# Attention and expert layer on one core: the attention part written out as a fixed order across two batches

## The chip, the core and the metric

The kernel runs on 1 core of one Trainium2 chip. The metric is the device time of one execution in microseconds (us). Four engines matter here: TensorE (PE) multiplies matrices into PSUM, VectorE (DVE) and ScalarE (ACT) work elementwise, and two queues issue transfers (DMA): SyncE's (SP) and GpSimd's (POOL). Each engine runs its own instructions strictly in the order in which they stand, and waits at each one until what it needs is there.

## What is computed

```python
# attention, for each batch b of 8 and head h of 8; 576 positions, 64 values a head
q_p, k_p = phi(q), phi(k)                 # phi(x) = max(x, 0) + exp(min(x, 0))
kv  = einsum('bhsd,bhse->bhde', k_p, v)
z   = sum(k_p, axis=2)
num = einsum('bhsd,bhde->bhse', q_p, kv)
den = einsum('bhsd,bhd->bhs', q_p, z)
x   = (num / den) as a matrix of 4608 x 512
# expert layer: 8 experts, 512 -> 1024 -> 512
P = exp(x @ w_gate)
for _ in range(8):                        # rows and columns made equal in turn
    P /= P.sum(1);  P /= P.sum(0);  P *= N / E
out = sum over e of P[:, e] * (relu(x @ w1[e]) @ w2[e])
```

## The kernel before

The work has three stages. The attention runs batch by batch (the loop at L103). The sinkhorn stage (L231 to L265) computes the 36 x 128 x 8 table of weights. The expert stage (L272 to L313) runs over four pairs of experts and nine blocks of 512 columns, with 16 tiles of `hps` (4 matmuls each) and 8 tiles of `yps` (8 matmuls each) for a block and a pair. The PE order begins the expert stage's `hps` right after the gate's matmuls (`lgps`, L234), between the matmuls of the sinkhorn stage.

Inside a batch the 576 positions stand in five chunks `c`, four of 128 rows and one of 64. This is what happens to a batch:

- SP loads k and q of each chunk (`kn`, `qn`, L134 and L138) in pieces of 256 bytes, POOL loads v (`vn`, L142) and casts it to 16 bits. `kn` and `qn` have 2 buffers, so the load of a chunk waits until DVE has used the chunk two before it. `vn` has 6.
- ACT computes exp(min(x, 0)) in two instructions each for k and q (`tk`, `tq`, L149, L150, L154, L155). DVE adds max(x, 0) (`kp`, `qp`, L151, L156). ACT casts `kp` to 16 bits (`kp16`, L153). PE sums it over the positions (`zps`, L158).
- After the fifth chunk DVE copies `zps` (`z_sb`, L160), PE spreads it over 128 rows (`zbc`, L161, in 32-bit numbers), and DVE normalises q chunk by chunk in four steps: product `jk` (L167), sum `den` (L169), reciprocal `rden` (L170), `qps` (L171).
- For each of four head pairs `i`, PE multiplies k and v (10 matmuls into `kvps`, L182), and DVE copies the two 64 x 64 blocks into `kv2` (L188, L190). `kvps` is one PSUM bank, so the matmuls of pair `i + 1` wait until the copies of pair `i` are done.
- PE transposes `qps` (4 matmuls into `qtr`, L196, one into `qtr4`, L200). ACT copies `qtr` to `qpsT` (L205), DVE copies `qtr4` (L207).
- PE multiplies `kv2` and `qpsT` (8 matmuls into `xps`, L217). ACT copies the tiles of even `i` (L220), DVE those of odd `i` (L223) into `xT`, which the expert stage reads.

The order on each engine is not the order of the code: a scheduler places every instruction by its own estimate of when it can run. It has put only a little of the next batch's `kp` and `qp` between the products of a batch. The weights of the first pair of experts (four loads, `load_pair_weights(0)`, L87) stand first on the POOL queue, ahead of all `vn`.

Of the kernel before, what the change touches and what calls it, by code (L numbers as in the profile page):

```python
# [8 lines left out]
FP32 = mybir.dt.float32  # L9
FP16 = mybir.dt.float16  # L10
A = mybir.AluOpType
# [10 lines left out]
def kernel(  # L22
# [49 lines left out]
    w2t = [w2p.tile([P, 2, NFT, DM], FP16, name=f"w2t{i}", tag="w2t")  # L72
           for i in range(NPAIR)]

    def load_pair_weights(pr):
        e0 = 2 * pr
        for j in range(2):
            nc.gpsimd.dma_start(  # L78
                out=w1t[pr][:, j],
                in_=moe_w1[e0 + j].rearrange("(dc di) f -> di dc f", di=P),  # L80
            )
            nc.gpsimd.dma_start(
                out=w2t[pr][:, j],
                in_=moe_w2[e0 + j].rearrange("(fc fi) d -> fi fc d", fi=P),
            )

    load_pair_weights(0)  # L87

    h_pair = hpp.tile([P, 2, NFT, NBW], FP16, name="h_pair")

# [9 lines left out]
    att = tc.alloc_tile_pool(name="att", bufs=1, side="right")  # L100
    apsum = tc.alloc_tile_pool(name="apsum", bufs=8, space=bass.MemoryType.PSUM)

    for b in range(B):  # L103
        kv2 = [att.tile([P, P], FP16, name=f"kv2_{b}_{i}", tag="kv2", bufs=8)
               for i in range(NHP)]
        qpsT = [att.tile([P, S], FP16, name=f"qpsT_{b}_{i}", tag="qpsT", bufs=8)
                for i in range(NHP)]
        kvps = apsum.tile([P, H, D], FP32, name=f"kvps_{b}", tag="aps")
        zps = apsum.tile([1, DM], FP32, name=f"zps_{b}", tag="aps")
        z_sb = att.tile([1, DM], FP32, name=f"z_sb_{b}", tag="z_sb", bufs=2)  # L110
        zbc = apsum.tile([P, DM], FP32, name=f"zbc_{b}", tag="aps")
        qtr4 = apsum.tile([P, NHP, SLAST], FP32, name=f"qtr4_{b}", tag="aps")

        kp = []
        kp16 = []
        vn = []
        qp = []
        qps = []
        for c in range(NCH):
            kp.append(att.tile([P, DM], FP32, name=f"kp_{b}_{c}", tag="kp", bufs=2))  # L120
            kp16.append(att.tile([P, DM], FP16, name=f"kp16_{b}_{c}", tag="kp16", bufs=6))
            vn.append(att.tile([P, DM], FP16, name=f"vn_{b}_{c}", tag="vn", bufs=6))
            qp.append(att.tile([P, DM], FP32, name=f"qp_{b}_{c}", tag="qp", bufs=6))
            qps.append(att.tile([P, DM], FP32, name=f"qps_{b}_{c}", tag="qps", bufs=6))

        for c in range(NCH):
            pc = P if c < NCH - 1 else SLAST
            s0 = c * P
            kn = att.tile([P, DM], FP32, name=f"kn_{b}_{c}", tag="kn", bufs=2)
            qn = att.tile([P, DM], FP32, name=f"qn_{b}_{c}", tag="qn", bufs=2)  # L130
            tmpk = att.tile([P, DM], FP32, name=f"tk_{b}_{c}", tag="tmpk", bufs=2)
            tmpq = att.tile([P, DM], FP32, name=f"tq_{b}_{c}", tag="tmpq", bufs=2)

            nc.sync.dma_start(  # L134
                out=kn[:pc].rearrange("p (h d) -> p h d", d=D),
                in_=k[b, :, s0 : s0 + pc, :].rearrange("h s d -> s h d"),
            )
            nc.sync.dma_start(  # L138
                out=qn[:pc].rearrange("p (h d) -> p h d", d=D),
                in_=q[b, :, s0 : s0 + pc, :].rearrange("h s d -> s h d"),  # L140
            )
            nc.gpsimd.dma_start(  # L142
                out=vn[c][:pc].rearrange("p (h d) -> p h d", d=D),
                in_=v[b, :, s0 : s0 + pc, :].rearrange("h s d -> s h d"),
            )
            if pc < P:
                nc.vector.memset(kn[pc:], 0.0)
                nc.vector.memset(qn[pc:], 0.0)
            nc.scalar.activation(tmpk, kn, AF.Relu, scale=-1.0)  # L149
            nc.scalar.activation(tmpk, tmpk, AF.Exp, scale=-1.0)  # L150
            nc.vector.scalar_tensor_tensor(out=kp[c], in0=kn, scalar=0.0,  # L151
                                           in1=tmpk, op0=A.max, op1=A.add)
            nc.scalar.activation(kp16[c], kp[c], AF.Copy)  # L153
            nc.scalar.activation(tmpq, qn, AF.Relu, scale=-1.0)  # L154
            nc.scalar.activation(tmpq, tmpq, AF.Exp, scale=-1.0)  # L155
            nc.vector.scalar_tensor_tensor(out=qp[c], in0=qn, scalar=0.0,  # L156
                                           in1=tmpq, op0=A.max, op1=A.add)
            nc.tensor.matmul(zps, ones16f[:pc], kp16[c][:pc],  # L158
                             start=(c == 0), stop=(c == NCH - 1))
        nc.vector.tensor_copy(out=z_sb, in_=zps)  # L160
        nc.tensor.matmul(zbc, ones32[0:1, :], z_sb[0:1, :], start=True, stop=True)  # L161

        for c in range(NCH):
            junk = att.tile([P, H, D], FP32, name=f"jk_{b}_{c}", tag="junk", bufs=2)
            den = att.tile([P, H], FP32, name=f"den_{b}_{c}", tag="den", bufs=2)
            rden = att.tile([P, H], FP32, name=f"rden_{b}_{c}", tag="rden", bufs=2)
            nc.vector.tensor_tensor(out=junk.rearrange("p h d -> p (h d)"),  # L167
                                    in0=qp[c], in1=zbc, op=A.mult)
            nc.vector.tensor_reduce(out=den, in_=junk, axis=AXX, op=A.add)  # L169
            nc.vector.reciprocal(out=rden, in_=den)  # L170
            nc.vector.scalar_tensor_tensor(  # L171
                out=qps[c].rearrange("p (h d) -> p h d", d=D),
                in0=qp[c].rearrange("p (h d) -> p h d", d=D), scalar=KXS,
                in1=rden.unsqueeze(2).to_broadcast([P, H, D]),
                op0=A.mult, op1=A.mult)

        for i in range(NHP):
            for j in range(2):
                hh = 2 * i + j
                for c in range(NCH):  # L180
                    pc = P if c < NCH - 1 else SLAST
                    nc.tensor.matmul(  # L182
                        kvps[:, hh, :],
                        kp16[c][:pc, i * P : (i + 1) * P],
                        vn[c][:pc, hh * D : (hh + 1) * D],
                        start=(c == 0), stop=(c == NCH - 1))
            nc.vector.memset(kv2[i].bitcast(FP32), 0.0)
            nc.vector.tensor_scalar(out=kv2[i][0:D, 0:D], in0=kvps[0:D, 2 * i, :],  # L188
                                    scalar1=0.0, scalar2=None, op0=A.add)
            nc.vector.tensor_scalar(out=kv2[i][D:P, D:P], in0=kvps[D:P, 2 * i + 1, :],  # L190
                                    scalar1=0.0, scalar2=None, op0=A.add)

        for i in range(NHP):
            qtr = apsum.tile([P, (NCH - 1) * P], FP32, name=f"qtr_{b}_{i}", tag="aps")
            for c in range(NCH - 1):
                nc.tensor.matmul(qtr[:, c * P : (c + 1) * P],  # L196
                                 qps[c][:, i * P : (i + 1) * P], idt,
                                 is_transpose=True,
                                 start=(c == 0), stop=(c == NCH - 2))
            nc.tensor.matmul(qtr4[:, i, :],  # L200
                             qps[NCH - 1][:SLAST, i * P : (i + 1) * P],
                             idt[:SLAST, :SLAST],
                             is_transpose=True,
                             start=(i == 0), stop=(i == NHP - 1))
            nc.scalar.activation(qpsT[i][:, 0 : (NCH - 1) * P], qtr, AF.Copy)  # L205
        for i in range(NHP):
            nc.vector.tensor_scalar(out=qpsT[i][:, (NCH - 1) * P : S],  # L207
                                    in0=qtr4[:, i, :],
                                    scalar1=0.0, scalar2=None, op0=A.add)

        for i in range(NHP):
            for sb in range(2):
                n0 = sb * NBW
                nw = NBW if sb == 0 else S - NBW
                xps = apsum.tile([P, nw], FP32, name=f"xps_{b}_{i}_{sb}",
                                 tag="aps")
                nc.tensor.matmul(xps, kv2[i], qpsT[i][:, n0 : n0 + nw],  # L217
                                 start=True, stop=True)
                if i % 2 == 0:
                    nc.scalar.activation(xT[i][:, b * S + n0 : b * S + n0 + nw],  # L220
                                         xps, AF.Copy)
                else:
                    nc.vector.tensor_scalar(  # L223
                        out=xT[i][:, b * S + n0 : b * S + n0 + nw], in0=xps,
                        scalar1=0.0, scalar2=None, op0=A.add)

    att.release()
    apsum.release()
# [115 lines left out]
```

## Time and profile before

| | |
|---|---|
| time, median of 4 runs | 1295.89 us (1294.96 to 1296.31) |
| the profiled execution: time, and its span | 1296.25 us, 1294.1 us |
| PE busy | 1148.2 us, 89% |
| DVE busy | 555.7 us, 43% |
| ACT busy | 359.8 us, 28% |

The span runs from the first to the last instruction; the execution's time holds 2.15 us besides. Shares over the whole span are a mean over unlike stages, so the rows below are taken stage by stage. A line of the profile that begins with a time gives start and duration in us, the engine, the line of the kernel, what is written and read, and how many instructions were merged into it. In square brackets it gives the idle time of the engine just before it and what ended that.

### The profile page before, as it was taken

The numbers are of one execution on the slowest core, as the hardware profiler recorded it, in microseconds if no ns is written. First come the engines' busy times: TensorE is split into PE (matmuls) and PEld (weight loads), VectorE is DVE, ScalarE is ACT, GpSimd is POOL, SyncE is SP. The second block draws the span as 40 slices with busy tenths as digits, with TensorE's granted clock in tenths as the row PEclk, the third lists the DMA queues.
The fourth block names the chain that finished last, engine by engine and source line by source line (L and its number), as shares of the span: only waits on it lengthen the run. The fifth ranks groups of instructions, "written<-read, shape, count | busy, mean of one in ns | idle before, by whom it ended". The sixth has DMA issues, their size and how long they took to land.

```text
span 1294.1 us, 13893 instructions
## 1 busy us (share of the span) xinstructions
PE 1148.2 (89%) x5658; PEld 529.2 (41%) x5658; DVE 555.7 (43%) x973; ACT 359.8 (28%) x627; POOL 48.2 (4%) x63
## 2 busy tenths in 40 slices
PE   0455555679999999999999999999999999999998
PEld 0222222245444444444444444444444444444443
DVE  1677767745333333333333333333334333333333
ACT  2566566521222111222112222112221112221111
POOL 3021111100000000100000001000000000000000
PEclk9999555569999999999999999999999999999999
DMA  9777766400000000520000007000000161000111
GB/s 185 109 96 99 102 105 103 64 1 2 1 1 1 1 1 1 82 49 1 1 1 1 1 1 131 1 1 1 1 1 1 32 119 45 33 33 33 41 49 41
DMA packets 130832, 50.71 MB, mean 39 GB/s; under 512 B 113872, under 2 KB 122064, under 8 KB 130768
## 3 DMA queue, kind: packets, MB, share of 16 engines
q0 software_dynamic: 50576, 21.51, 13.6%
q1 hardware_dynamic: 80192, 28.32, 9.1%
q8 instruction: 44, 0.72, 0.2%
q14 instruction: 20, 0.16, 0.0%
HBM read 61.88 MB, written 9.44 MB: 55 GB/s over the span
## 4 chain that ended last, share of the span: by engine, by line
PE 84%; DVE 8%; DMA 4%; ACT 3%; issue 1%; SPq 0%
PE hps L282 39%; PE yps L298 38%; DMA qn<-in_q_dram 2%; PE qtr L196 2%; DVE jk L167 2%; DVE den L169 2%; DVE qps L171 2%; DMA kn<-in_k_dram 2%; PE zbc L161 1%; PE kvps L182 1%; ACT kp L153 1%; PE xps L217 1%; PE qtr L200 1%; DVE kp L151 1%; PE vps L254 1%
## 5 line engine op out<-in xcount | busy, mean ns | idle before, releaser
L282 PE MATMUL hps<-xT,w1t 128*128 128x512 f16 x2304 | 507.1, 380 | 0.0
L298 PE MATMUL yps<-w2t,h_pair 128*128 128x512 f16 x2304 | 504.0, 379 | 0.4 <-DVE out_acc L304 0.4
L287 ACT ACTIVATE h_pair<-hps 128x512 f16<-128x512 f32 x360 | 214.7, 597 | 778.6 <-PE hps L282 756.8
L298 PEld LDWEIGHTS <-h_pair 128*128 128x128 f16 x2304 | 225.1, 98 | 271.6 <-issue 0.7
L282 PEld LDWEIGHTS <-w1t 128*128 128x128 f16 x2304 | 224.8, 98 | 270.5 <-issue 2.2
L308 DVE SCALAR_TENSOR_TENSOR out_acc<-yps,pnat,out_acc 128x512 f32<-128x512 f32 x252 | 189.2, 751 | 246.3 <-PE yps L298 246.3
L289 DVE TENSOR_SCALAR h_pair<-hps 128x512 f16<-128x512 f32 x216 | 149.2, 691 | 333.7 <-PE hps L282 333.6
L158 PE MATMUL zps<-kp,ones16f 128*1 128x512 f16 (+1 forms) x40 | 21.0, 581 | 79.0 <-ACT kp L153 79.0
L196 PE MATMUL qtr<-idt,qps 128*128 128x128 f32 x128 | 43.9, 447 | 43.4 <-DVE qps L171 41.5
L196 PEld LDWEIGHTS qtr<-idt,qps 128*128 128x128 f32 x128 | 22.7, 204 | 54.7 <-DVE qps L171 47.9
L205 ACT ACTIVATE qpsT<-qtr 128x512 f16<-128x512 f32 x32 | 19.1, 597 | 84.6 <-PE qtr L196 84.6
L182 PE MATMUL kvps<-vn,kp 128*128 128x64 f16 (+1 forms) x320 | 34.3, 239 | 8.8 <-DVE kv L190 8.8
L304 DVE TENSOR_SCALAR out_acc<-yps,pnat 128x512 f32<-128x512 f32 x36 | 26.9, 750 | 33.7 <-PE yps L298 33.7
L142 POOL DMA_DIRECT2D vn<-in_v_dram x40 | 33.6, 865 | 208.9 <-PE kvps L182 199.1
L182 PEld LDWEIGHTS <-kp 128*128 128x128 f16 (+1 forms) x320 | 26.1, 124 | 31.9 <-issue 23.2
L151 DVE SCALAR_TENSOR_TENSOR kp<-kn,tk 128x512 f32<-128x512 f32 x40 | 27.2, 681 | 23.8 <-ACT tk L150 23.6
L156 DVE SCALAR_TENSOR_TENSOR qp<-qn,tq 128x512 f32<-128x512 f32 x40 | 27.3, 682 | 18.5 <-ACT tq L155 18.2
L78 POOL DMA_DIRECT2D w1t<-in_moe_w_dram x8 | 6.1, 763 | 749.0 <-PE hps L282 749.0
L158 PEld LDWEIGHTS <-ones16f 128*1 128x1 f16 (+1 forms) x40 | 3.1, 91 | 74.6 <-issue 72.3
L167 DVE TENSOR_TENSOR jk<-qp,zbc 128x512 f32<-128x512 f32 x40 | 25.9, 681 | 9.8 <-PE zbc L161 9.8
L149 ACT ACTIVATE tk<-kn 128x512 f32<-128x512 f32 x40 | 24.9, 622 | 17.5 <-DMA kn<-in_k_dram 17.5
L154 ACT ACTIVATE tq<-qn 128x512 f32<-128x512 f32 x40 | 24.9, 624 | 14.6 <-DMA qn<-in_q_dram 14.5
(52 smaller groups left out, 310.9 us busy)
## 6 DMA issues: line engine op xcount, KB each, us to landing
out_dram<-out_acc SPq DMA_DIRECT2D x36, 256.0 KB, 2.0
kn<-in_k_dram SPq DMA_DIRECT2D x32, 256.0 KB, 3.6
qn<-in_q_dram SPq DMA_DIRECT2D x32, 256.0 KB, 3.3
w1t<-in_moe_w_dram POOLq DMA_DIRECT2D x8, 1024.0 KB, 11.4
w2t<-in_moe_w_dram POOLq DMA_DIRECT2D x8, 1024.0 KB, 13.7
vn<-in_v_dram POOLq DMA_DIRECT2D x32, 128.0 KB, 4.3
kn<-in_k_dram SPq DMA_DIRECT2D x8, 128.0 KB, 3.6
qn<-in_q_dram SPq DMA_DIRECT2D x8, 128.0 KB, 3.4
```

Source lines behind the costliest of these rows:

```text
L142: nc.gpsimd.dma_start(out=vn[c][:pc].rearrange("p (h d) -> p h d", d=D), in_=v[b, :, s0 : s0 + pc, :].rearrange("h s d -> s h d"),)
L151: nc.vector.scalar_tensor_tensor(out=kp[c], in0=kn, scalar=0.0, in1=tmpk, op0=A.max, op1=A.add)
L156: nc.vector.scalar_tensor_tensor(out=qp[c], in0=qn, scalar=0.0, in1=tmpq, op0=A.max, op1=A.add)
L167: nc.vector.tensor_tensor(out=junk.rearrange("p h d -> p (h d)"), in0=qp[c], in1=zbc, op=A.mult)
L182: nc.tensor.matmul(kvps[:, hh, :], kp16[c][:pc, i * P : (i + 1) * P], vn[c][:pc, hh * D : (hh + 1) * D], start=(c == 0), stop=(c == NCH - 1))
L196: nc.tensor.matmul(qtr[:, c * P : (c + 1) * P], qps[c][:, i * P : (i + 1) * P], idt, is_transpose=True, start=(c == 0), stop=(c == NCH - 2))
L282: nc.tensor.matmul(hps, w1t[pr][:, j, c, ft * P : (ft + 1) * P], xT[c][:, n0 : n0 + NBW], start=(c == 0), stop=(c == NHP - 1))
L287: nc.scalar.activation(h_pair[:, j, ft, :], hps, AF.Relu)
L289: nc.vector.tensor_scalar(out=h_pair[:, j, ft, :], in0=hps, scalar1=0.0, scalar2=None, op0=A.max)
L298: nc.tensor.matmul(yps, h_pair[:, j, fc, ti * P : (ti + 1) * P], w2t[pr][:, j, fc, :], start=(fc == 0), stop=(fc == NFT - 1))
L304: nc.vector.tensor_scalar(out=out_acc[:, t, :], in0=yps, scalar1=pcol, scalar2=None, op0=A.mult)
L308: nc.vector.scalar_tensor_tensor(out=out_acc[:, t, :], in0=yps, scalar=pcol, in1=out_acc[:, t, :], op0=A.mult, op1=A.add)
```

## The change

The attention loop is replaced by small functions, one for each piece of work, and by `step(b)`, which calls them in a fixed order. Inside `tc.manual_schedule` the order on DVE, PE and POOL is now the order of the code; ACT and SP are still placed by the scheduler. A step holds work of three batches: the normalising of batch b, the products, transposes and outputs of batch b - 1, and `kp`, `qp`, `zps` of batch b + 1. Nine steps run, of which the first has no b - 1, the eighth no b + 1, and the ninth only the products and outputs of the last batch.

`kn`, `qn`, `tmpk`, `tmpq` get 4 buffers instead of 2, `kp` 3 instead of 2, and `kp16`, `vn`, `qp`, `qps` 10 instead of 6. The fifth chunk's elementwise work covers 64 rows, so its two memsets (L147, L148) are gone. The first pair's weights are issued in the step b = 6, behind all `vn`, and the two `w1` ahead of the two `w2`.

```diff
-    load_pair_weights(0)
...
-    for b in range(B):
...
-            kn = att.tile([P, DM], FP32, name=f"kn_{b}_{c}", tag="kn", bufs=2)
+            kn = att.tile([P, DM], FP32, name=f"kn_{b}_{c}", tag="kn", bufs=4)
...
-            if pc < P:
-                nc.vector.memset(kn[pc:], 0.0)
-                nc.vector.memset(qn[pc:], 0.0)
...
+    def step(b):
+        m, n = b < B, b + 1 < B
+        o = 0 <= b - 1
+        if m:
+            z_bcast(b)
+        if n:
+            emit_A1(b + 1)
+            if b + 1 == B - 1:
+                for ld in (load_w1, load_w2):
+                    ld(0, 0)
+                    ld(0, 1)
+            dve_in(b + 1, 0)
+        if m:
+            jk(b, 0); jk(b, 1)
+        if o:
+            kv_ms(b - 1)
+            pe_kv(b - 1, 0); kv_cp(b - 1, 0)
+            pe_tr(b - 1, 0)
+        if m:
+            dn(b, 0); dn(b, 1); rd(b, 0); rd(b, 1); qs(b, 0)
+        if o:
+            pe_kv(b - 1, 1); kv_cp(b - 1, 1)
+            pe_tr(b - 1, 1)
+        if m:
+            qs(b, 1); jk(b, 2); jk(b, 3)
+        if o:
+            pe_kv(b - 1, 2); kv_cp(b - 1, 2)
+            pe_tr(b - 1, 2)
+        if m:
+            dn(b, 2); dn(b, 3); rd(b, 2); rd(b, 3); qs(b, 2)
+        if o:
+            pe_kv(b - 1, 3); kv_cp(b - 1, 3)
+            pe_tr(b - 1, 3)
+        if m:
+            qs(b, 3); jk(b, 4)
+        if o:
+            qT4(b - 1)
+            for i in range(NHP):
+                pe_x(b - 1, i)
+        if m:
+            dn(b, 4)
+        if o:
+            x_cp(b - 1, 1)
+        if m:
+            rd(b, 4)
+            qs(b, 4)
+        if o:
+            x_cp(b - 1, 3)
+        if n:
+            for c in range(1, NCH):
+                dve_in(b + 1, c)
+            pe_z(b + 1)
+
+    with tc.manual_schedule(engines={mybir.EngineType.DVE, mybir.EngineType.PE,
+                                    mybir.EngineType.Pool}):
+        emit_A1(0)
+        dve_in(0, 0)
...
+        for b in range(B + 1):
+            step(b)
```

The functions keep the instructions of before: `emit_A1` the loads and ACT's `tk`, `tq`; `dve_in` `kp`, `qp` and ACT's `kp16`; `z_bcast` `z_sb` and `zbc`; `jk`, `dn`, `rd`, `qs` the four steps of normalising; `pe_kv`, `kv_cp` the products and their copies; `pe_tr`, `qT4` the transposes and DVE's copies of `qtr4`; `pe_x`, `x_cp` the outputs and DVE's copies of them.

On DVE, around the products of batch 3, this stands before (the first number in a name is the batch, and the number behind the last _ is only a count of buffers):

```order
L188 TENSOR_SCALAR kv2_3_2_899<-kvps_3_905 64x64
L190 TENSOR_SCALAR kv2_3_2_899<-kvps_3_905 64x64
L156 SCALAR_TENSOR_TENSOR qp_4_1_1178<-qn_4_1_1211,tq_4_1_1213 128x512
L188 TENSOR_SCALAR kv2_3_3_900<-kvps_3_905 64x64
L190 TENSOR_SCALAR kv2_3_3_900<-kvps_3_905 64x64
L207 TENSOR_SCALAR qpsT_3_0_901<-qtr4_3_909 128x64
```

and this on DVE after, at the same products, in the step b = 4:

```order
L226 TENSOR_SCALAR kv2_3_2_640<-kvps_3_646 64x64
L228 TENSOR_SCALAR kv2_3_2_640<-kvps_3_646 64x64
L192 TENSOR_REDUCE den_4_2_1307<-jk_4_2_1306 128x8
L192 TENSOR_REDUCE den_4_3_1311<-jk_4_3_1310 128x8
L196 RECIPROCAL rden_4_2_1308<-den_4_2_1307 128x8
L196 RECIPROCAL rden_4_3_1312<-den_4_3_1311 128x8
L201 SCALAR_TENSOR_TENSOR qps_4_2_931<-qp_4_2_926,rden_4_2_1308 128x512
L226 TENSOR_SCALAR kv2_3_3_641<-kvps_3_646 64x64
L228 TENSOR_SCALAR kv2_3_3_641<-kvps_3_646 64x64
```

Between the copies of two head pairs there now stand four or five instructions of the following batch, where one stood.

On ACT, at the last chunk of a batch, this stands before:

```order
L153 ACTIVATE kp16_3_4_931<-kp_3_4_930 128x512
L154 ACTIVATE tq_3_4_998<-qn_3_4_996 128x512
L155 ACTIVATE tq_3_4_998<-tq_3_4_998 128x512
L149 ACTIVATE tk_4_0_1197<-kn_4_0_1195 128x512
L150 ACTIVATE tk_4_0_1197<-tk_4_0_1197 128x512
```

and this on ACT after, in the step b = 3:

```order
L163 ACTIVATE kp16_4_3_917<-kp_4_3_912 128x512
L148 ACTIVATE tk_5_0_1194<-kn_5_0_1192 128x512
L163 ACTIVATE kp16_4_4_918<-kp_4_4_913 64x512
L149 ACTIVATE tk_5_0_1194<-tk_5_0_1194 128x512
L150 ACTIVATE tq_5_0_1195<-qn_5_0_1193 128x512
L151 ACTIVATE tq_5_0_1195<-tq_5_0_1195 128x512
```

The first instruction on the next batch's k now stands ahead of the cast of the last chunk, on which `zps` and `z_sb` wait.

On POOL the weights stood first:

```order
L78 DMA w1t0_90<-in_moe_w1_dram 128x4x1024
L82 DMA w2t0_94<-in_moe_w2_dram 128x8x512
L78 DMA w1t0_90<-in_moe_w1_dram 128x4x1024
L82 DMA w2t0_94<-in_moe_w2_dram 128x8x512
L142 DMA vn_0_0_132<-in_v_dram 128x8x64
```

and stand behind the last batch's v after:

```order
L144 DMA vn_7_2_1695<-in_v_dram 128x8x64
L144 DMA vn_7_3_1696<-in_v_dram 128x8x64
L144 DMA vn_7_4_1697<-in_v_dram 64x8x64
L76 DMA w1t0_90<-in_moe_w1_dram 128x4x1024 x2
L82 DMA w2t0_94<-in_moe_w2_dram 128x8x512 x2
```

The four loads moved past all 40 loads of v. Behind the gate's matmuls (`lgps`), the order on PE, DVE and ACT is the same in both kernels, instruction by instruction.

## Rows read from the trace of the kernel before

**Rows 1.** Busy us (instructions) of each engine, clock, DMA share, GB/s, in two stretches

```profile
44.08:254.40 210.32, 118.05 (x525) 56.87 (x525) 153.67 (x367) 124.12 (x231) 28.48 (x34) 0.71 0.65 95
281.10:1294.10 1013.00, 1008.63 (x4913) 459.74 (x4912) 378.93 (x547) 214.75 (x361) 9.83 (x12) 1.00 0.10 22
```

**Rows 2.** Timeline of PE: from the gate's matmuls into the expert stage

```profile
276.64 4.01 PE L234 MATMUL lgps<-wg,xT 128*128 128x8 f16 x144 [0.86 <-DVE xT L223]
...
281.10 4.06 PE L282 MATMUL hps<-xT,w1t 128*128 128x512 f16 x10
...
286.92 1.90 PE L282 MATMUL hps<-xT,w1t 128*128 128x512 f16 x8
```

**Rows 3.** Timelines: ACT's last wait ahead of DVE's first z_sb, and z_sb

```profile
42.26 0.63 ACT L154 ACTIVATE tq<-qn 128x512 f32<-128x512 f32 x1 [1.52 <-DMA qn<-in_q_dram]
...
44.08 0.68 DVE L160 COPY z_sb<-zps 1x512 f32<-1x512 f32 x1 [2.62 <-PE zps L158]
```

**Rows 4.** DMA view of 0 to 50 us: packets; issues, KB each, median us to landing

```profile
DMA packets 23968, 8.60 MB, mean 172 GB/s; under 512 B 20896, under 2 KB 22944, under 8 KB 23968
...
kn<-in_k_dram SPq DMA_DIRECT2D x7, 256.0 KB, 6.3
```

**Rows 5.** DMA view of 60 to 260 us: loads of k

```profile
kn<-in_k_dram SPq DMA_DIRECT2D x24, 256.0 KB, 3.5
```

**Rows 6.** Timeline of DVE: the normalising of one batch

```profile
194.16 0.68 DVE L160 COPY z_sb<-zps 1x512 f32<-1x512 f32 x1 [1.33 <-PE zps L158]
...
197.00 1.28 DVE L167 TENSOR_TENSOR jk<-qp,zbc 128x512 f32<-128x512 f32 x2 [1.57 <-PE zbc L161]
...
199.63 1.28 DVE L171 SCALAR_TENSOR_TENSOR qps<-qp,rden 128x512 f32<-128x512 f32 x2
200.83 1.28 DVE L167 TENSOR_TENSOR jk<-qp,zbc 128x512 f32<-128x512 f32 x2
```

**Rows 7.** Timeline of DVE: the copies at the end of that batch

```profile
213.82 0.22 DVE L188 TENSOR_SCALAR kv<-kvps 64x64 f16<-64x64 f32 x1 [2.77 <-PE kvps L182]
...
214.30 0.62 DVE L207 TENSOR_SCALAR qpsT<-qtr 128x64 f16<-128x64 f32 x4
215.26 1.78 DVE L223 TENSOR_SCALAR xT<-xps 128x512 f16<-128x512 f32 x4 [0.34 <-PE xps L217]
```

**Rows 8.** DMA view of 186 to 196 us: busy tenths in 40 slices, packets

```profile
DMA  1479999999999999999999988999766799999950
...
DMA packets 8337, 1.52 MB, mean 152 GB/s; under 512 B 8336, under 2 KB 8336, under 8 KB 8336
```

**Rows 9.** Timeline of PE: transposes, products and outputs of one batch

```profile
150.36 1.11 PE L196 MATMUL qtr<-idt,qps 128*128 128x128 f32 x4
151.41 0.36 PE L200 MATMUL qtr<-idt,qps 64*128 64x64 f32 x1
...
152.61 1.08 PE L182 MATMUL kvps<-vn,kp 128*128 128x64 f16 x10
...
153.78 2.36 PE L217 MATMUL xps<-qpsT,kv 128*128 128x512 f16 x8
```

**Rows 10.** Timeline of ACT and of PE: from the last cast to zbc

```profile
192.86 0.63 ACT L153 ACTIVATE kp<-kp 128x512 f16<-128x512 f32 x1 [0.84 <-DVE kp L151]
...
194.89 2.07 PE L161 MATMUL zbc<-z_sb,ones 1*128 1x512 f32 x2 [0.77 <-DVE z_sb L160]
```

**Rows 11.** Timeline of POOL: the v loads of one batch

```profile
213.75 4.19 POOL L142 DMA_DIRECT2D vn<-in_v_dram  x5 [24.89 <-PE kvps L182]
```

**Rows 12.** The page's DMA issues: weights, median us to landing

```profile
w1t<-in_moe_w_dram POOLq DMA_DIRECT2D x8, 1024.0 KB, 11.4
w2t<-in_moe_w_dram POOLq DMA_DIRECT2D x8, 1024.0 KB, 13.7
```

**Rows 13.** As rows 1, two stretches with a change of clock

```profile
190.00:192.00 2.00, 0.38 (x1) 0.08 (x1) 1.19 (x3) 2.00 (x4) 0.00 (x0) 1.00 1.59 146
284.00:286.00 2.00, 2.00 (x40) 1.21 (x38) 0.00 (x0) 0.60 (x1) 0.00 (x0) 0.84 0.00 0
```

## The prediction made before the run

> **What bounds the kernel now.** I read the busy time by stage first. From 281.10 us to the end PE is busy 1008.6 of 1013.0 us [rows 1]: the expert stage is bound by PE and does nothing else. Behind the gate's matmuls the order on PE, DVE and ACT is the same in both kernels, so whatever moves the start of `lgps`, now 276.64 us [rows 2], moves the end by as much, as long as the weights are there. The whole question is when `lgps` starts.
>
> In the attention no engine is full. From the first `z_sb` to the last, 210.3 us, DVE is busy 153.7, ACT 124.1, PE 118.1, and the DMA share is 0.65 [rows 1]. The reader is to see a chain that walks from engine to engine. Two stretches make it up. The first is the start: `z_sb` of batch 0 runs at 44.08 us, behind a wait for the last q at 42.26 [rows 3]. In these 50 us k takes 6.3 us from issue to landing [rows 4], later 3.5 [rows 5]; the weights are the other transfer under way. The second is the period of a batch. `z_sb` of batch 5 runs at 194.16 [rows 6], so a batch takes (194.16 - 44.08) / 5 = 30.0 us. In each, DVE stands idle 1.33 us for `zps`, 1.57 for `zbc` [rows 6] and 2.77 for the products [rows 7], and PE stands idle while DVE normalises. I then read DVE's timeline row by row for the price of each instruction.
>
> **The start.** k and q of batch 0 are 9 full chunks of 1024 pieces each, 9216 packets. The weights are no longer ahead on POOL, but with 10 buffers v of batches 0 and 1 goes out at once, another 9216 packets of the same pieces. Where only these kinds run, 8337 packets take about 38 slices of 0.25 us, 9.5 us [rows 8], or 880 a us. Both queues together need 18432 / 880 = 21 us; with 2 us until the first packets flow the last q lands at 23. From there to `z_sb` it takes 44.08 - 42.26 = 1.8 us [rows 3]: `z_sb` of batch 0 at about 24.5 instead of 44.1. Bounds: if k and q did not share with v, 14; if the rate stayed at that of the first 50 us, 23968 / 50 = 480 a us [rows 4], 42. I take 24.5 because rows 8 are the same two kinds of packets.
>
> **A full step (b = 1 to 6).** DVE's prices, start to start: 0.60 us for an instruction of 512 columns (two `qps` in 200.83 - 199.63), 3.83 for `jk`, `den`, `rden`, `qps` of two chunks (200.83 - 197.00) [rows 6], 0.48 for the two copies of a head pair (214.30 - 213.82), 0.62 for the four copies of `qtr4`, 1.78 for the four of `xps` [rows 7]. The four memsets of `kv2` I put at 0.1 each, an estimate below the 0.22 of a copy with as many columns [rows 7]. A step is then `z_sb` 0.60, ten `kp`, `qp` 6.00, 2.5 pairs of chunks 9.57, copies of products 1.92, memsets 0.40, `qtr4` 0.62, `xps` 1.78: 20.9 us. The fifth chunk with 64 rows I count in full, since no row shows one; the two memsets that go are left out.
>
> Now the waits. I set `jk` of chunk 0 at 0.
>
> - Products. PE starts the first pair's at about 0 and needs 1.0 us for ten matmuls and 1.4 for a set of transposes [rows 9], so the four pairs end at 1.0, 3.4, 5.8 and 8.2. By the prices above DVE comes to their copies at 1.6, 4.1, 6.4 and 8.9, so the 2.77 us of rows 7 go. PE waits for the copies of the pair before, done at 2.1, 4.6, 6.9: about when its transposes end, so neither waits. The copies of `qtr4` begin at 10.6, the `xps` take 2.4 us [rows 9] and end near 13.2, and DVE ends its copies at 14.3.
> - `z_sb`. DVE does `kp` and `qp` of chunks 1 to 4 from 14.3 to 19.1. The next batch's first k goes into the buffer that `kp` of chunk 1 sets free at 15.0, and lands 3.5 us later [rows 5], at 18.5. On ACT its `tk` stands ahead of the last `kp16`. That cast therefore starts at 19.1, and `z_sb` 1.30 us after it (194.16 - 192.86) [rows 6, 10], at 20.4. This is a new wait of 1.3 us on DVE; queued behind ACT's `tk` are the cast, `zps`, `z_sb`, and behind that everything.
> - `zbc`. From `z_sb` to `jk` it takes 197.00 - 194.16 = 2.84 us [rows 6], and DVE has 1.8 us of work there: 1.0 us idle.
>
> So a step is 20.4 + 2.8 = 23.2 us. If the load lands early enough to cost nothing it is 21.9; if it takes the 6.3 us of rows 4 it is 26.0. I take 3.5, the row of the same transfer beside v alone. ACT has no other wait for loads: the eight go out as the buffers come free and are there some 10 us before DVE asks for them.
>
> **The sum.** Step 0 lacks the parts of the batch before it, 4.7 us: 18.5. So `z_sb` of batch 1 is at 43.0, of batch 7 at 43.0 + 6 x 23.2 = 182.2, and `jk` of batch 7 at 185.0. The step b = 7 runs PE to 13.2 as above. Then the last batch's products and outputs follow with nothing to lie beside: four times 1.0 + 1.4, the first copy of `qtr4` 0.25, the `xps` 2.4, the last two copies 0.9: 26.3 us after `jk`. In the kernel before, this piece lay partly inside the normalising; here it hangs over, and that is in the sum. `lgps` starts at 211.3 instead of 276.6, 65.3 us earlier. The profiled execution took 1296.25 us (0.4 above the median of the four runs, so the two can stand for each other): 1296.25 - 65.3 = **1231 us**.
>
> The four weight loads leave POOL's queue behind v of batch 7, which waits for the products of batch 5 at 8.2 in the step b = 6, at 170 us, and takes 4.2 us to issue [rows 11]. One after another they need 11.4 + 11.4 + 13.7 + 13.7 = 50 us from 174 [rows 12]: both `w1` by 197, both `w2` by 224. The first `hps` comes at 216 (281.10 - 276.64 behind `lgps`) [rows 2]. The first `yps` comes 64 matmuls later, at no less than 1.90 / 8 each [rows 2], at 231. The move costs nothing there; without this cover every us of delay would be paid in full.
>
> **The rivals.**
>
> *The clock rises earlier.* Up to 284 the rows show TensorE at the lower of its two levels, 1.2 GHz: ten `hps` in 4.06 us, later eight in 1.90 [rows 2], and the granted clock goes up within 284 to 286 [rows 13], when PE has had no gap since `lgps`. In the changed kernel PE has no gap above 1 us from `zbc` of batch 7 on, so it may be at 2.4 GHz for the last batch's products. That halves 9.6 us of products and transposes down to where DVE's copies limit it (about 4.5 us less), and ten `hps` by 1.7: 1225 us. Against it: around 190 a rise is granted too [rows 13], and at 194.89 `zbc` still takes 2.07 us [rows 10]. The Trainium skill ("TensorE: Matmul & The Clock Gate", Part 1) says that "the default state is throttled, and activity releases the throttle"; by that rule this rival holds, and rows 13 agree at 284.
>
> *The loads hold each step.* Transfers now have 23 us for what filled 0.65 of 30, so k may land late, and ACT holds the last cast for it. With 6.3 us instead of 3.5 [rows 4, 5] a step is 26.0: 1231 + 6 x 2.8 = 1248 us.
>
> *The overlap doesn't come.* The scheduler's order already put some `kp` and `qp` between the products. If a step stays at 30.0 us, only the start is won: 1231 + 6 x 6.8 = 1272 us. Against it: DVE's 20.9 us are counted from rows.
>
> *Slower: lockstep.* With DVE and PE in a fixed order a late product stops both. If each of the four copies waited 2.77 us and each of the three copies behind them 0.34 [rows 7], a step would be 23.2 + 12.1 = 35.3 us: 1231 + 6 x 12.1 = 1304 us. It is slower from 34.1 us a step on. Against it: by the prices above PE is ahead of DVE by 0.6 to 0.7 us at each copy, and DVE's idle time would have to pass 11 us.
>
> **How the numbers follow.** Forecast 0.45, with its own range of 1225 to 1240 (start 20 to 30, step 22.5 to 24); earlier clock 0.27; loads 0.18; no overlap 0.07; lockstep 0.02; 0.01 for no change. A measurement of this kernel can tell 0.2%, 2.6 us, from no change. All cases but the last two are faster by more: 0.97, within 0.01, slower 0.02. The range reaches from the early clock with a start of 17 (1217) to the loads with a start of 33 (1257). It leaves out the last three cases and the ends of the others.
>
> **What would show it.** `z_sb` of batch 0 near 24.5, then every 23.2 us. On DVE no wait for products above 0.5 us, about 1.3 for `zps` and 1.0 for `zbc`. `lgps` near 211, and 1017 us from there to the end. The forecast is wrong if k lands later than 4.5 us after its issue, if DVE waits for PE between its copies, or if `hps` waits for `w1t`.

## The result and the profile after

The changed kernel takes 1230.01 us (median of 8 runs, 1228.63 to 1230.64), the kernel before 1296.11 us (12 runs): a ratio of 0.949, 95% interval 0.948 to 0.950. The profiled execution took 1230.11 us with a span of 1228.3 us.

Two stretches of the changed kernel, from the first `z_sb` to the last and from `lgps` to the end (columns as in [rows 1]):

```profile
27.62:183.34 155.72, 103.78 (x457) 48.40 (x457) 141.39 (x339) 118.72 (x222) 28.43 (x34) 1.00 0.98 130
211.12:1228.30 1017.18, 1012.77 (x5058) 464.10 (x5058) 378.94 (x547) 215.13 (x361) 9.76 (x12) 1.00 0.10 22
```

The second row is the one of before over again: 1012.8 us of PE in 1017.2. In the first, DVE is busy 141.4 of 155.7 us, 91%, where it was 73% [rows 1]. What DVE waits for in that stretch (line, releaser; us in total, times, longest), the three largest of before:

```profile
DVE kv L188 <- PE kvps L182: 21.8, 14, 2.8
DVE z_sb L160 <- PE zps L158: 10.6, 7, 2.6
DVE jk L167 <- PE zbc L161: 8.3, 7, 1.6
...
```

and of the changed kernel, whole:

```profile
DVE z_sb L174 <- PE zps L169: 5.8, 7, 1.0
DVE jk L186 <- PE zbc L175: 5.4, 6, 1.0
DVE qp L161 <- ACT tq L151: 2.7, 3, 1.2
```

With the two next of before, for `tk` and `tq` (5.2 and 4.4), 50 us of waits have become 14. Those for the products are gone. DVE's timeline, at the first two steps, a full one and the last:

```profile
27.62 0.67 DVE L174 COPY z_sb<-zps 1x512 f32<-1x512 f32 x1
...
46.25 0.68 DVE L174 COPY z_sb<-zps 1x512 f32<-1x512 f32 x1 [0.74 <-PE zps L169]
...
114.95 0.68 DVE L174 COPY z_sb<-zps 1x512 f32<-1x512 f32 x1 [1.00 <-PE zps L169]
...
117.79 1.28 DVE L186 TENSOR_TENSOR jk<-qp,zbc 128x512 f32<-128x512 f32 x2 [0.96 <-PE zbc L175]
...
183.34 0.68 DVE L174 COPY z_sb<-zps 1x512 f32<-1x512 f32 x1 [0.73 <-PE zps L169]
186.18 1.28 DVE L186 TENSOR_TENSOR jk<-qp,zbc 128x512 f32<-128x512 f32 x2 [2.16 <-PE zbc L175]
```

These answer to [rows 6]: the first step takes 18.6 us and the six full ones (183.34 - 46.25) / 6 = 22.85 us each, where a batch took 30.0. PE at the end of the attention, the answer to [rows 2]:

```profile
208.16 2.10 PE L263 MATMUL xps<-qpsT,kv 128*128 128x512 f16 x8
211.12 4.00 PE L349 MATMUL lgps<-wg,xT 128*128 128x8 f16 x144 [0.86 <-DVE xT L273]
215.05 0.59 PE L357 MATMUL bbc<-ones 1*128 1x8 f32 x2
215.58 3.75 PE L397 MATMUL hps<-xT,w1t 128*128 128x512 f16 x10
```

`lgps` starts 65.5 us earlier, and `hps` follows it without a wait for `w1t`: the weights were there.

### The profile page after: what moved, and what is told of

The parts are those of the page before. It is cut to its first block, busy times and chain, and to the rows that moved or that the text cites. A ratio compares the mean times of both kernels' runs of the same rounds, so it can differ in the third digit from the quotient of the medians.

```text
span 1228.3 us, 13873 instructions
## 1 busy us (share of the span) xinstructions
PE 1144.4 (93%) x5658; PEld 527.7 (43%) x5658; DVE 546.4 (44%) x957; ACT 358.3 (29%) x627; POOL 48.1 (4%) x63
## 4 chain that ended last, share of the span: by engine, by line
PE 85%; DVE 10%; DMA 3%; ACT 1%; issue 1%; SPq 0%; DVEq 0%
PE hps L397 41%; PE yps L413 41%; DMA kn<-in_k_dram 2%; DVE jk L186 2%; DVE den L192 2%; DVE qps L201 2%; PE zbc L175 1%; DMA qn<-in_q_dram 1%; DVE xT L273 1%; PE vps L369 1%; DVE kp L159 1%; DVE kv L228 1%; DVE z_sb L174 0%; ACT kp L163 0%; DVE rden L196 0%
## 5 line engine op out<-in xcount | busy, mean ns | idle before, releaser
L236 PE MATMUL qtr<-idt,qps 128*128 128x128 f32 x128 | 35.6, 431 | 0.0
L161 DVE SCALAR_TENSOR_TENSOR qp<-qn,tq 128x512 f32<-128x512 f32 (+1 forms) x40 | 27.1, 677 | 11.5 <-ACT tq L151 11.5
L217 PEld LDWEIGHTS <-kp 128*128 128x128 f16 (+1 forms) x320 | 22.5, 117 | 21.4 <-issue 10.8
L159 DVE SCALAR_TENSOR_TENSOR kp<-kn,tk 128x512 f32<-128x512 f32 (+1 forms) x40 | 27.0, 675 | 9.7 <-ACT tk L149 9.7
L163 ACT ACTIVATE kp<-kp 128x512 f16<-128x512 f32 (+1 forms) x40 | 24.9, 624 | 18.1 <-DVE kp L159 18.0
L186 DVE TENSOR_TENSOR jk<-qp,zbc 128x512 f32<-128x512 f32 (+1 forms) x40 | 26.0, 682 | 7.7 <-PE zbc L175 7.5
L201 DVE SCALAR_TENSOR_TENSOR qps<-qp,rden 128x512 f32<-128x512 f32 (+1 forms) x40 | 27.2, 685 | 0.6
L148 ACT ACTIVATE tk<-kn 128x512 f32<-128x512 f32 (+1 forms) x40 | 24.8, 620 | 5.9 <-DMA kn<-in_k_dram 5.7
```

Of the source, the lines that this page charges most:

```text
L159: nc.vector.scalar_tensor_tensor(out=d["kp"][c][r], in0=d["kn"][c][r], scalar=0.0, in1=d["tmpk"][c][r], op0=A.max, op1=A.add)
L161: nc.vector.scalar_tensor_tensor(out=d["qp"][c][r], in0=d["qn"][c][r], scalar=0.0, in1=d["tmpq"][c][r], op0=A.max, op1=A.add)
L186: nc.vector.tensor_tensor(out=junk[: PCS[c]].rearrange("p h d -> p (h d)"), in0=d["qp"][c][: PCS[c]], in1=d["zbc"][: PCS[c]], op=A.mult)
L201: nc.vector.scalar_tensor_tensor(out=d["qps"][c][: PCS[c]].rearrange("p (h d) -> p h d", d=D), in0=d["qp"][c][: PCS[c]].rearrange("p (h d) ...
L217: nc.tensor.matmul(d["kvps"][:, hh, :], d["kp16"][c][:pc, i * P : (i + 1) * P], d["vn"][c][:pc, hh * D : (hh + 1) * D], start=(c == 0), st ...
L236: nc.tensor.matmul(qtr[:, c * P : (c + 1) * P], qps[c][:, i * P : (i + 1) * P], idt, is_transpose=True, start=(c == 0), stop=(c == NCH - 2))
```

## The experiments

All times are medians, each with its ratio to the kernel before and the 95% interval.

**e1: the late weights alone**, in the kernel before.

```diff
-    load_pair_weights(0)
...
+    with tc.manual_schedule(engines={mybir.EngineType.Pool}):
         for b in range(B):
...
+            if b == B - 1:
+                load_pair_weights(0)
             nc.vector.tensor_copy(out=z_sb, in_=zps)
```

> The kernel before, with one part of the change: the four weight loads of the first pair stand behind v of the last batch on POOL's queue. Buffers and the order on DVE and PE stay those of before. Theory (the start and the period are separate terms): z_sb of batch 0 near 27.6 us as in the changed kernel instead of 44.1, the period of a batch still near 30.0 us, so 1296.1 - 16.5 = about 1280 us. Rival 1 (with two buffers for k and q the first batch is held by its own chain and not by the shared transfers): z_sb of batch 0 above 35 us, 1288 us or more. Rival 2 (the late weights are not hidden here): hps waits for w1t, 1290 us or more.

1281.67 us, 0.9894 (0.9878 to 0.9911). The time fits, its parts less well. `z_sb` of batch 0 is at 24.24, 19.8 us earlier, and the period stays at (233.55 - 24.24) / 7 = 29.9 us. But from the last `z_sb` to `lgps` it takes 27.8 us, before 22.2 (254.40 to 276.64) [rows 1, 2], because q of the last batch now goes out among the weights: SP issues it at 229.1, behind the first two weight loads of POOL (227.7 and 228.4), and it lands 10.9 us later. DVE's timeline of that run:

```profile
233.55 0.68 DVE L162 COPY z_sb<-zps 1x512 f32<-1x512 f32 x1 [1.33 <-PE zps L158]
241.33 0.69 DVE L156 SCALAR_TENSOR_TENSOR qp<-qn,tq 128x512 f32<-128x512 f32 x1 [7.10 <-ACT tq L155]
```

So the start is worth 20 us by itself, and with two buffers some 5.5 of them are given back at the end.

**e2: late weights and more buffers, the code's order as before.**

```diff
-            kp16.append(att.tile([P, DM], FP16, name=f"kp16_{b}_{c}", tag="kp16", bufs=6))
+            kp16.append(att.tile([P, DM], FP16, name=f"kp16_{b}_{c}", tag="kp16", bufs=10))
...
-            kn = att.tile([P, DM], FP32, name=f"kn_{b}_{c}", tag="kn", bufs=2)
+            kn = att.tile([P, DM], FP32, name=f"kn_{b}_{c}", tag="kn", bufs=4)
...
```

> The run with the late weights, and the changed kernel's numbers of buffers (kp 3, kp16, vn, qp, qps 10, kn, qn, tmpk, tmpq 4), but the body of the loop written as before and ordered by the scheduler. Theory (the buffers only make room, the gain is in the order): the products still stand behind the normalising of their own batch, and DVE's reductions and PE's products still take turns, so a period falls only by loads that come earlier, to 28 to 29 us: about 1280 - 7 x 1.5 = 1270 us. Rival (buffers alone release the overlap): a period near 23 us, 1235 us or less.

1257.19 us, 0.9703 (0.9689 to 0.9718): neither theory. The period is (214.23 - 24.89) / 7 = 27.0 us. DVE's waits from the first `z_sb` to the last, of e1:

```profile
DVE kv L190 <- PE kvps L184: 21.8, 14, 2.8
DVE z_sb L162 <- PE zps L158: 10.7, 8, 1.3
DVE jk L169 <- PE zbc L163: 7.7, 7, 1.6
```

and of e2:

```profile
DVE kv L190 <- PE kvps L184: 17.6, 14, 2.2
DVE z_sb L162 <- PE zps L158: 4.3, 5, 1.7
...
DVE jk L169 <- PE zbc L163: 3.1, 4, 1.0
```

With room, the scheduler runs `kp` and `qp` of the next batch beside the chain of `z`, and those waits fall by 11 us. Those for the products mostly stay: that part does need the written order. From the last `z_sb` to `lgps` it takes 22.3 us again (214.23 to 236.48), so with the larger numbers of buffers the 5.5 us that e1 gave back at the end are kept. I had given the buffers too little.

**e3: the new code, but DVE and PE ordered by the scheduler.**

```diff
-    with tc.manual_schedule(engines={mybir.EngineType.DVE, mybir.EngineType.PE,
-                                    mybir.EngineType.Pool}):
+    with tc.manual_schedule(engines={mybir.EngineType.Pool}):
```

> The changed kernel, but only POOL's queue keeps the written order; on DVE and PE the scheduler orders the same code. Its order on DVE is almost the written one; on PE it puts three sets of transposes ahead of the second pair's products. Theory (in the changed kernel PE is only 0.6 us ahead of DVE at each copy, so an order that puts 3 us of transposes first makes DVE wait): the second pair's products end 6.5 us after jk of chunk 0 instead of 3.4, DVE comes to the copy at 4.1 and waits 2.4 us; less 0.4 for the memsets that move into idle time, 2.0 a step: z_sb every 24.9 us and 1230 + 7 x 2.0 = 1244 us. Rival (DVE has slack that takes this up, or the written order itself is of no account): no wait above 0.5 us at the copies, 1230 us.

1243.49 us, 0.9596 (0.9581 to 0.9610), as the theory had it: full steps of (194.66 - 44.65) / 6 = 25.0 us. One wait a step on DVE, at the second pair's copy:

```profile
125.64 0.68 DVE L201 SCALAR_TENSOR_TENSOR qps<-qp,rden 128x512 f32<-128x512 f32 x1
128.80 0.22 DVE L226 TENSOR_SCALAR kv<-kvps 64x64 f16<-64x64 f32 x1 [2.48 <-PE kvps L217]
```

This is the lockstep rival in small: the order on PE decides, and a lead of PE of only some 0.8 us at this copy (in the changed kernel products done at 121.06, copied at 121.87) is lost by transposes put ahead. The start (`z_sb` of batch 0 at 25.98) and the end (29.8 us from the last `z_sb` to `lgps`) differ by -1.6 and +2.1 us and nearly cancel.

**e4: the weights first again**, in the changed kernel.

```diff
+    load_pair_weights(0)
...
-            if b + 1 == B - 1:
-                for ld in (load_w1, load_w2):
-                    ld(0, 0)
-                    ld(0, 1)
```

> The changed kernel with the weight loads of the first pair ahead of all v on POOL's queue, as in the kernel before; all else as changed. Theory (the start is won by the weights' absence alone): z_sb of batch 0 back near 44 us, full steps still near 22.9, so 1230 + 16.5 = 1246 us, or a few us more if v of batch 0 comes late for its products. Rival (the other buffers and the order give the start too): z_sb of batch 0 below 35 us, 1236 us or less.

1247.64 us, 0.9630 (0.9616 to 0.9645). `z_sb` of batch 0 is at 43.75, the full steps take 22.8 us. The start and the step are separate terms.

**e5: v held until k and q of batch 0 are there.**

```diff
+        if b == 0:
+            hold = att.tile([P, 1], FP32, name="hold", tag="hold", bufs=1)
+            nc.gpsimd.tensor_copy(out=hold[:SLAST], in_=d["qn"][NCH - 1][:SLAST, 0:1])
+        for c in range(NCH):
...
             nc.gpsimd.dma_start(
```

> The changed kernel with one copy of 64 values on POOL ahead of the first v, which reads the last q of batch 0: v of batches 0 and 1 goes out only when k and q of batch 0 are there. Theory (the start is longer than the transfer of k and q because v shares the 16 engines with them): alone the last q lands near 13 us, and ACT becomes the limit: its 25 instructions of 0.55 us behind the first k at 4.6 put z_sb of batch 0 at about 18.5 us instead of 27.6; v of batch 0 is there before its products, so 1230 - 9 = 1221 us. Rival 1 (k and q have a pace of their own): z_sb of batch 0 stays above 25 us, 1228 us or more. Rival 2 (v comes late for the products of batch 0 and gives the gain back): PE waits for vn in the step of batch 1, 1226 us or more.

1222.71 us, 0.9428 (0.9414 to 0.9442). `z_sb` of batch 0 is at 20.05: ACT is the limit, as the theory had it, but needs 3.1 us a chunk and not 5 x 0.55: it waits 0.24 us for `kp` in each. PE waits for no v (rival 2). The DMA view shows the sharing. In the changed kernel from 9 to 20 us (queue, kind: packets, MB, share):

```profile
q0 software_dynamic: 6094, 0.77, 107.5%
q1 hardware_dynamic: 4050, 1.02, 66.8%
```

and in e5, with k and q alone, from 5 to 12 us:

```profile
q1 hardware_dynamic: 6045, 1.52, 138.6%
```

Alone k and q move 6045 / 7 = 864 packets a us, beside v 4050 / 11 = 368, and both together 922. The Trainium skill ("DMA: Bandwidth & Descriptors", Issuing engines are not separate DMA queues) says that DMAs of all issuing engines run on the same 16 engines and interleave; these rows agree.

**e6: kp before qp at the end of a step.** `dve_k` and `dve_q` are `dve_in` in two parts: `kp` with its cast, and `qp`.

```diff
-            for c in range(1, NCH):
-                dve_in(b + 1, c)
+            dve_in(b + 1, 1)
+            for c in range(2, NCH):
+                dve_k(b + 1, c)
             pe_z(b + 1)
+            for c in range(2, NCH - 1):
+                dve_q(b + 1, c)
...
             z_bcast(b)
+            if b > 0:
+                dve_q(b, NCH - 1)
```

> The changed kernel with another order at the end of a step on DVE: kp 1, qp 1, kp 2, kp 3, kp 4, qp 2, qp 3, then z_sb, then qp 4, and kp and qp of chunk 0 of the next batch as before; the sums of kp16 on PE follow kp 4. On ACT the last kp16 then stands ahead of the next batch's first tk. Theory (the wait for zps is the chain kp 4, cast, sums on PE, 2.0 us, with 0.6 us of work beside it; the load of k adds 0.3): DVE has work through the whole chain, z_sb comes 4.4 us after kp 1 instead of 5.9, jk of chunk 0 1.5 us earlier, 1.5 x 7 = 10 us: about 1220 us, and waits for zps below 0.3 us a step. Rival (the loads of the next batch's first k and q hold the step, as the second part of the wait for zps was forecast): the wait goes over to kp and qp of chunk 0, 1227 us or more.

1219.48 us, 0.9408 (0.9394 to 0.9422). DVE's timeline, from `kp` of chunk 1 to `jk`:

```profile
104.01 0.67 DVE L159 SCALAR_TENSOR_TENSOR kp<-kn,tk 128x512 f32<-128x512 f32 x1
...
108.42 0.68 DVE L182 COPY z_sb<-zps 1x512 f32<-1x512 f32 x1
...
110.45 0.69 DVE L166 SCALAR_TENSOR_TENSOR qp<-qn,tq 128x512 f32<-128x512 f32 x1
111.26 1.29 DVE L194 TENSOR_TENSOR jk<-qp,zbc 128x512 f32<-128x512 f32 x2
```

`z_sb` comes 4.41 us after `kp` and waits for nothing; a full step is (173.01 - 43.83) / 6 = 21.53 us, 1.32 less: the wait for `zps` (0.83) is gone, and most of the one for `zbc`, which now has `qp` of the last chunk beside it. No load took the place of the wait. `z_sb` of batch 7 comes 10.3 us earlier, 8.9 of them by the steps; 1.4 are the start (26.23), which is nearly as early in e10 (26.45) without an edit there. In this profile the clock rose earlier, too. PE, in the products of the last batch:

```profile
188.44 1.06 PE L225 MATMUL kvps<-vn,kp 128*128 128x64 f16 x10
189.43 1.11 PE L244 MATMUL qtr<-idt,qps 128*128 128x128 f32 x4
...
190.89 0.76 PE L225 MATMUL kvps<-vn,kp 128*128 128x64 f16 x10
191.59 0.66 PE L244 MATMUL qtr<-idt,qps 128*128 128x128 f32 x4
...
202.06 4.45 PE L410 MATMUL hps<-xT,w1t 128*128 128x512 f16 x10
```

From 190.9 us on the same matmuls are faster, and the last `z_sb` to `lgps` takes 24.8 us instead of 27.8. Then ten `hps` take 4.45 us, 0.7 more than in the changed kernel. This profiled execution took 1217.42 us, the other three 1219.1 to 1221.2.

**e7: both.** The edits of e5 and e6.

> The changed kernel with both edits: v held until k and q of batch 0 are there, and kp before qp at the end of a step. Theory: the start and the step are separate terms and add up, 1230 - 9 - 10 = 1211 us, with z_sb of batch 0 near 18.5 us and a full step near 21.4 us. Rival (with shorter steps the 16 DMA engines become the limit): k lands later than 6 us after its issue, the step stays above 22.3 us, 1217 us or more.

1213.83 us, 0.9359 (0.9344 to 0.9375). `z_sb` of batch 0 at 20.25, full steps of 21.54 us: they add up but for the 1.4 us of start in e6, and the engines of the DMA hold nothing back (k lands 4.4 us after its issue, the median from 60 to 160 us). Of the 2.8 us by which the sum was missed, 1.75 are the start.

**e8: two buffers for k, q, tk, tq.**

```diff
-            kn = att.tile([P, DM], FP32, name=f"kn_{b}_{c}", tag="kn", bufs=4)
+            kn = att.tile([P, DM], FP32, name=f"kn_{b}_{c}", tag="kn", bufs=2)
...
```

> The changed kernel with two buffers instead of four for each of kn, qn, tmpk and tmpq, as before; order and all other buffers as changed. Theory (a load's 4 to 5 us from issue to landing stands on the chain as soon as its buffer comes free only inside the same step): the third and fourth k go out behind kp of chunk 1 and 2 and land 4 us later, so kp 3 starts 5.7 us after kp 1 instead of 2.4, kp 4 at about 8.1 instead of 3.6, and jk of the next step some 5.7 us later: a full step of 28.5 us, 1230 + 7 x 5.7 = 1270 us. Rival (loads are hidden by the reorder alone, the four buffers bring nothing): a step of 22.9, 1230 us.

1285.01 us, 0.9914 (0.9899 to 0.9929). The steps are as expected, 27.9 us, with `kp` of chunk 3 5.2 us after that of chunk 1. But the last, from 190.65 to 237.09, takes 46.4: SP issues the last two k and q of batch 7 from 208.5 on, behind POOL's weights (from 205.6 on). DVE's timeline of it:

```profile
208.97 0.68 DVE L159 SCALAR_TENSOR_TENSOR kp<-kn,tk 128x512 f32<-128x512 f32 x1
...
224.43 0.69 DVE L159 SCALAR_TENSOR_TENSOR kp<-kn,tk 128x512 f32<-128x512 f32 x1 [14.18 <-ACT tk L149]
231.53 0.69 DVE L161 SCALAR_TENSOR_TENSOR qp<-qn,tq 128x512 f32<-128x512 f32 x1 [6.41 <-ACT tq L151]
```

**e9: the same, the weights held until the last q of batch 7 is there.**

```diff
+                wh = att.tile([P, 1], FP32, name="wh", tag="wh", bufs=1)
+                nc.gpsimd.tensor_copy(out=wh[:SLAST],
+                                      in_=ST[B - 1]["qn"][NCH - 1][:SLAST, 0:1])
                 for ld in (load_w1, load_w2):
```

> The run with two load buffers, and a copy on POOL of 64 values of batch 7's last q ahead of the weight loads, so that no weight goes out before the last q has landed. Theory (in that run the step of batch 7 took 46.4 us and the others 27.9 because k and q of batch 7 went out among the weights): all steps 27.9 us, so 1285 - 18.5 = 1266.5 us, the weights still in time for hps. Rival 1 (the long step has another cause): it stays above 40 us, 1285 us. Rival 2 (the held weights come too late for hps or yps): 1275 us or more, with PE waiting for w1t or w2t.

1266.15 us, 0.9767 (0.9753 to 0.9780). All full steps take 28.0 us. `hps` waits for no weights (rival 2). So the long step was k and q among the weights: 18.9 us of e8.

**e10: PE filled.** The results of the added matmuls are not used.

```diff
+    def warm(n):
+        d = ST[B - 1]
+        for _ in range(n):
+            nc.tensor.matmul(d["zbc"], d["kp16"][0][:, 0:P], d["kp16"][0],
+                             start=True, stop=True)
...
+            if b == B - 1:
+                warm((5, 1, 1, 1, 2)[c])
...
+            if (b, i, sb) in ((B - 3, 0, 0), (B - 2, 0, 0)):
+                warm(2)
```

> The changed kernel with 14 more matmuls of 512 columns on PE, whose results are written into zbc of the last batch ahead of its own value: 2 in the wait for qpsT in each of the last two steps, 10 between and behind the sums of z of the last batch. PE then has no gap above about 0.5 us from 172 us on. Theory (the clock goes up when PE has worked long enough without a gap; in the run with k before q it went up at 190.9 us, within the last batch's products, and z_sb of batch 7 to lgps took 24.8 us instead of 27.8): the products of the last batch take 0.7 to 0.8 us for ten instead of 1.03, lgps starts 3 us earlier or more, 1227 us or less. Rival (what PE does in these 15 us does not decide it): products of the last batch at 1.03, 1230 us; 1231 us if the added matmuls delay zbc.

1226.36 us, 0.9472 (0.9456 to 0.9488); the interval overlaps that of the changed kernel, but four of its five runs (1225.92 to 1226.99) lie below all eight of it, the fifth at 1231.31. PE in its profile:

```profile
175.23 1.25 PE L168 MATMUL zbc<-kp 128*128 128x512 f16 x5
177.87 0.38 PE L175 MATMUL zps<-kp,ones16f 128*1 128x512 f16 x1 [1.39 <-ACT kp L163]
...
181.85 1.03 PE L168 MATMUL zbc<-kp 128*128 128x512 f16 x2
...
184.82 1.05 PE L225 MATMUL kvps<-vn,kp 128*128 128x64 f16 x10
...
200.51 0.77 PE L225 MATMUL kvps<-vn,kp 128*128 128x64 f16 x10 [0.56 <-DVE kv L236]
...
211.78 4.30 PE L407 MATMUL hps<-xT,w1t 128*128 128x512 f16 x10
```

and the granted clock there (last column but two):

```profile
184.00:198.00 14.00, 12.87 (x71) 7.37 (x70) 12.39 (x35) 3.28 (x7) 0.00 (x0) 0.50 1.16 199
198.00:210.00 12.00, 10.31 (x170) 7.68 (x169) 5.91 (x26) 4.32 (x10) 0.00 (x0) 0.93 0.02 3
210.00:216.00 6.00, 6.00 (x62) 3.07 (x59) 1.69 (x5) 1.60 (x3) 0.00 (x0) 0.52 0.01 3
```

The clock is up within the added matmuls (five in 1.25 us; at the lower level two take 1.03), falls near 181.8 behind 2.9 us of gaps in 5.5, rises again near 198.7 and falls near 209, within `lgps`. So the fill left more idle time than was planned: the longest gap there is 1.39 us, and not 0.5. The last `z_sb` to `lgps` takes 25.5 us instead of 27.8, and ten `hps` 0.55 longer: 1.8 us gained. The other 1.4 us by which `lgps` comes earlier lie ahead of the last `z_sb`, 1.2 of them in the start, which this edit leaves as it was:

```profile
26.45 0.67 DVE L182 COPY z_sb<-zps 1x512 f32<-1x512 f32 x1
```

So the theory's 3 us from the clock are not reached. Nor is it certain that the filling caused the rise. Of the ten profiles of the new code, only e10 and e11 rise ahead of the last `z_sb`; but e6 rises within the last products with nothing filled, and e4, e5 and e9 at the very end (`lgps` in 3.8 us instead of 4.0, ten `hps` in 4.45). Single executions of e5, e7 and e9 lie 2.5 to 2.9 us below their median.

**e11: both edits, and PE filled.**

> The same 14 matmuls in the kernel with both edits (v held, kp before qp). Theory: as in the other, 3 us or more below the 1213.8 of that kernel, 1210.5 us. Rival: 1214 us, last products at 1.03 us for ten.

1213.17 us, 0.9363 (0.9350 to 0.9376): not to be told from e7 by its time, so the theory's 1210.5 is missed. In its profile the last `z_sb` to `lgps` takes 24.4 us (167.51 to 191.90) instead of the 27.8 of e7, with the last products at 0.77 us; but `z_sb` itself comes 0.6 us later, and ten `hps` take 4.26 us instead of 3.80.

## Why the prediction was right, point by point

- **The start, 24.5 forecast, 27.62 measured.** The mechanism is shown by e4 (43.75 with the weights ahead) and e5 (20.05 without v). The rate was right: 922 packets a us against 880 taken from [rows 8]. The term was sized too small by 3.1: the last q landed at 25.3, not 23, and `z_sb` came 2.3 us behind it, not 1.8. The 0.5 is the written order: DVE does `qp` of the last chunk ahead of `z_sb` (27.01, then 27.62), while in e2 and e3, where the scheduler orders DVE, it is 1.82 us (23.07 to 24.89, 24.16 to 25.98). The 2.3 of the landing: up to 25.3 us the two queues had moved 20768 packets, not 18432: 1648 more of k and q (batch 1) and 688 more on POOL's queue. At 880 a us these make 23.6 us, with the first 2 us 25.6. No run took these packets away, so that they caused the delay is not shown, and part of it is scatter: with the same loads and buffers the last q lands at 24.1 in e10 and at 23.1 in e2.
- **Step 0, 18.5 forecast, 18.63 measured.**
- **A full step, 23.2 forecast, 22.85 measured.** DVE's work came out at 22.85 - 0.83 - 0.9 = 21.1 us (20.9 forecast); the fifth chunk with 64 rows costs as much as the others (`kp` 0.67 us), as I had counted it. DVE waits for no product in steps 0 to 6. `zbc` cost 0.9 (1.0 forecast). `zps` cost 0.83 (5.8 us in 7) instead of 1.3.
- **The cause of that wait was wrong.** I put the 1.3 us down to k's landing, with ACT's `tk` ahead of the last cast. ACT's timeline, and the loads of k between 30 and 180 us:

```profile
113.13 0.63 ACT L148 ACTIVATE tk<-kn 128x512 f32<-128x512 f32 x1 [0.32 <-DMA kn<-in_k_dram]
113.67 0.61 ACT L163 ACTIVATE kp<-kp 64x512 f16<-64x512 f32 x1
...
kn<-in_k_dram SPq DMA_DIRECT2D x24, 256.0 KB, 4.7
```

  DVE ends `kp` of chunk 4 at 113.34, so the load and `tk` delay the cast by 0.33 us only. The rest of the wait is the chain itself, `kp`, cast, sum, `z_sb`, which has just 0.6 us of `qp` beside it. The last of these waits shows it: no next batch follows, the cast starts at 182.04, right behind `kp`, and `z_sb` at 183.34 still waits 0.73. So of 0.73 to 1.00 us a step the load adds at most 0.27. My own sign of being wrong, k later than 4.5 us after its issue, was met (4.7, the median) without harm: the k on this chain is the first of its batch and lands about 3.4 us after its issue (109.76 to 113.13), as forecast. The forecast's "if the load lands early enough a step is 21.9" was therefore wrong, and e6 shows it: the order of `kp` and `qp` took the wait away with the loads as they were. The landing does cost much where the buffers are few (e8, e9: 28.0 us a step).
- **The end, 26.3 us behind the last `jk` forecast, 24.9 measured:** step 7 ended 0.6 us earlier, the last outputs 0.6, the products 0.2.
- **The sum.** 24.5 + 18.5 + 6 x 23.2 + 2.8 + 26.3 = 211.3, measured 211.12. Single terms were off by +3.1, +0.1, -2.1 and -1.4 us, so the agreement within 1 us is luck: errors of +3.2 and -3.5 cancel. The start alone scatters by 1.2 us between executions (27.62 here, 26.45 in e10).
- **The weights** were hidden, as forecast. What I did not see is why: the four load buffers let k and q of batch 7 go out before the weights (SP issues the last q at 164.6, POOL the first weight at 175.6). With two (e1, e8) the move costs 5.5 and 18.9 us. The weights landed sooner than the 50 us that I had allowed, one after another: side by side, `w1` 11.7 and `w2` 20.3 us after their issue (medians).
- **The rivals.** An earlier clock did not come about in the profile of the changed kernel, where the last products take 1.03 us for ten, but it occurs: e6 and e10 show it for the same matmuls, worth 2.3 to 3.4 us up to `lgps` (e11 too), of which the slower `hps` give 0.5 to 0.7 back. I had priced it at 6, with no fall behind it, and on the condition that PE has no gap above 1 us from `zbc` of batch 7 on. The changed kernel has one of 1.23 ahead of 197.29; e6 has the same gap (1.24) and the clock rose behind it. By the Trainium skill's rule ("TensorE: Matmul & The Clock Gate", Part 1) that activity releases the throttle, the filled PE should rise; in e10 it did, and fell again within `lgps`, which PE runs without a gap. What decides when is open. The loads did not hold the step (e7: 21.5 us with the same loads). The overlap came. The lockstep did not, and e3 shows a small case of it: 13 us from one wait of 2.5 us a step.

## What to carry to other kernels

Size a pipelined step on the engine that walks through all of it, and then walk every chain that leaves this engine and comes back (here `kp`, cast, sum, `z_sb`): what counts is how much of its own work lies beside the chain, and a change of order alone can fill it (some 9 us here). A large load that is moved behind small ones is hidden only if the small ones are really issued first; count the buffers that let them. Two queues share the DMA engines, so at the start of a kernel hold back what the first result does not need (7 us here); with e7 the changed kernel goes from 1230 to 1213.8 us.

## What was not expected of the hardware

- With both queues at work, POOL's casting loads got 554 and SP's 368 of 922 packets a us. In bytes it is the other way round: 0.77 MB and 1.02 MB in 11 us, 163 GB/s together, where k and q alone moved 218.
- The granted clock of the profile reads 1.00 through the whole changed kernel, while ten products last 1.03 to 1.06 us; in e10, at 0.50 on record, they last the same 1.03 to 1.05, and at 1.00 0.77. So up to some 216 us the 1.00 of the changed kernel is not a measured level; the durations are.
- The clock fell again near 209 us in e10, within `lgps`, behind 10.3 us at the higher level in which PE was busy 8.6, and came back near 216.
